# Sparse attention and a mixer MLP on one core: the later batches' instruction order, from fixed delays to a recorded reckoning of the engines

## The chip, the core and the metric

The kernel runs on one core of a Trainium2 chip. A core has a matrix engine (TensorE, PE in the profile), three engines for elementwise work (VectorE or DVE, ScalarE or ACT, GpSimd or POOL) and SyncE (SP), which issues most of the DMAs here. Each engine takes its own instructions strictly in the order in which the program lists them, and waits for others by semaphores. The metric is the device time of one execution in microseconds; lower is better.

## The reference

`q`, `k` and `v` are [4, 8, 768, 64] (batch, head, position, width of a head). Attention is masked by blocks of 32 positions.

```python
scores = scale * np.matmul(q, k.transpose(0, 1, 3, 2))      # scale = 1/8
mask = np.abs(blk_i - blk_j) <= 1                           # neighbours, first and last block,
mask = mask | (blk_i == 0) | (blk_j == 0) | (blk_i == n_blocks - 1) | (blk_j == n_blocks - 1)
...                                                         # and 3 sampled blocks for each block
attn = softmax(np.where(mask, scores, -1e9))
x = np.matmul(attn, v)        # heads side by side: [4, 768, 512]
h = x.transpose(0, 2, 1) @ U @ V                            # rank 32, over positions
u = x + h.transpose(0, 2, 1)
out = u + np.maximum(u @ w_ch1, 0.0) @ w_ch2                # 512 -> 2048 -> 512
```

## The kernel before

Heads are handled in pairs: 4 batches x 4 pairs make 16 pairs, numbered `i`. The scores of a pair are cut into nine **units** `u`, each 128 keys (or two halves of them) by 512 queries for both heads. A unit is a few matmuls into a double bank of PSUM (`psc`), one exp on ScalarE (`est<-psc`, 128 x 1024) and, in batches 1 to 3, one multiplication by a 0/1 mask on VectorE (`mask_mul`, `est<-est,m`). After the nine units of a pair come

- `values`: 72 small matmuls into `pav`, a reciprocal and a scaling on VectorE (`xs`), and a cast to 16 bits on GpSimd (`xh`);
- `mix_a_rows`: 12 matmuls into `pa` with `Ut` (from U), and two small VectorE steps (`a16`);
- `mix_h_rows`: 6 matmuls into `ph` with `Vd` (from V), an add on VectorE (`xf`), a cast on GpSimd (`uh`), and `turn_u`, a DMA that transposes `uh` into `uT`.

When all four pairs of a batch have their `uT`, its MLP can run: 16 blocks of the first layer (`w1`, tile `pt`), each in two phases of eight matmuls with a relu after the second, on ScalarE or VectorE (`tT<-pt`); then the second layer (`w2_rows`, tile `pch`, 192 matmuls for a batch), each third of it followed by an add on VectorE (`leave`, tile `of`) and a store. The matmuls of batches 0 to 2 use half of the rows each, two at a time; the last batch's (`w2`, and `w1` with whole rows) use all rows. Batch 0's attention is a part of its own (the head, its masks are added inside the matmul, and ScalarE sets its pace); its MLP runs beside batch 1's attention, and so on; the last MLP runs alone.

PSUM holds four double banks in the later part, numbered 0 to 3 and handed out by `double` and `give_back`: `psc`, `pt`, `pch`, `pav`, `pa` and `ph` all take one.

The order of every engine's instructions is that in which the Python code records them (`keep`). In before, the later batches are recorded in **groups of one unit**, numbered `gi`. Unit `gi` is recorded; then the masks of the units before it; when the ninth mask of a pair is recorded, its `values` goes one group later, `mix_a_rows` five and `mix_h_rows` eight groups later (`work`, `beside`); then a share of the running MLP (`run_fill`), such that it is used up when the next MLP opens. The MLPs open at fixed groups: 5 for the first, and then 16 groups after the last unit of the batch (`OPENS`, `LATE`). `clk` holds a reckoned time for each engine; it chooses banks, and ScalarE or VectorE for a relu.

```python
OPENS = [5]
for b in range(1, B):
    last = [n for n, gr in enumerate(groups) if (HP * b + HP - 1, NU - 1) in gr][0]
    OPENS.append(last + LATE)
...
work.append((gi + 1, steps[0]))      # values
beside.append((gi + 5, steps[1]))    # mix_a_rows
beside.append((gi + 8, steps[2]))    # mix_h_rows and turn_u
...
run_fill(sum(c for c, _, _ in fill) / (to_come[0] - gi))
```

Loads of `q`, `k` and `v` (`issue`) go out on SP three pairs ahead and are cast on GpSimd (`cast`) two pairs ahead; `turn_dma` transposes q and k of the next pair by DMA. U and V are loaded into a part of `w2t`'s space on SP, after the loads of pair 2, and copied into `Ut` and `Vt` on GpSimd at the start of pair 1 (`at_unit`, lines 877 and 883), ahead of the first `xh` casts.

Of the kernel before, what the change touches and what calls it, by code (L numbers as in the profile page):

```python
# [21 lines left out]
def kernel(  # L22
# [81 lines left out]
    clk = {"pe": 0.0, "act": 0.0, "dve": 0.0}  # L104
# [21 lines left out]
    def give_back(t, when):  # L126
        n = held.pop(id(t))[0]
        doubles[n] = (doubles[n][0], when + LAG)

# [296 lines left out]
    ready = {}  # L426
# [10 lines left out]
    def scores(i, u, est):  # L437
        psc = double("psc", len(exp_end) % 2 if i < HP else None)
        for g, q0, q1, at in parts(u):
            kc = slice(g * P, (g + 1) * P)  # L440
            for h in range(2):
                o = psc[:, h, at : at + q1 - q0]
                if i < HP:
                    s = i % 2
                    mm(o, ka[s][h][:, kc], qa[s][h][:, q0:q1], True, True)
                else:
                    qT, kT = (qkT[i, nm].rearrange(flat) for nm in "qk")
                    mm(o, kT[rows[h], kc], qT[rows[h], q0:q1], True, True)
        clk["pe"] += 0.22
        if i < HP:  # L450
            clk["pe"] = max(clk["pe"], exp_end[-2]) + 0.1
        keep(nc.scalar.activation(out=est, in_=psc, func=AF.Exp, scale=0.125))  # L452
        exp_end.append(run_on("act", 0.905))
        ready[id(est)] = exp_end[-1]
        give_back(psc, exp_end[-1])

    def mask_mul(u, est):
# [8 lines left out]
        run_on("dve", 0.8, ready[id(est)])  # L466
# [49 lines left out]
    def values(i, ests, xs, xh):  # L516
# [3 lines left out]
        for c in range(2):  # L520
            for h in range(2):
# [8 lines left out]
        rcp = misc.tile([P, 2, 6], FP32, tag="rcp", name="rcp")  # L530
        keep(nc.vector.reciprocal(out=rcp, in_=pv[:, :, :, D]))  # L531
        keep(
            nc.vector.tensor_tensor(  # L533
                out=xs.rearrange("p (c j) (h d) -> p c (j h) d", c=2, h=2),
                in0=pv[:, :, :, 0:D],
                in1=rcp[:, :, :, None].broadcast_to([P, 2, 6, D]),
                op=ALU.mult,
            )
        )
        give_back(pav, run_on("dve", 1.2))  # L540
        keep(nc.gpsimd.tensor_copy(out=xh, in_=xs))  # L541
# [11 lines left out]
    def mix_a_rows(xh, box):  # L553
# [8 lines left out]
        a16 = box["a"] = misc.tile([P, P], FP16, tag="a16", name="a16")  # L562
        keep(nc.vector.tensor_copy(out=a16, in_=pa[:, 0, 0:P]))
        keep(nc.vector.tensor_tensor(out=a16, in0=a16, in1=pa[:, 1, 0:P], op=ALU.add))
        give_back(pa, run_on("dve", 0.57))
# [27 lines left out]
    def mix_h_rows(i, a16, xs, uh):  # L593
# [3 lines left out]
        for j in range(3):  # L597
            for c in range(2):
# [4 lines left out]
        u = xfs[b][:, :, hp * P : (hp + 1) * P]  # L603
        keep(
            nc.vector.tensor_tensor(  # L605
                out=u.rearrange("p (c j) n -> p c j n", c=2),
                in0=xs.rearrange("p (c j) n -> p c j n", c=2),
                in1=ph[:, :, 0:HS].rearrange("p c (j n) -> p c j n", j=3),
                op=ALU.add,
            )  # L610
        )
        give_back(ph, run_on("dve", 0.9))
        keep(nc.gpsimd.tensor_copy(out=uh, in_=u))  # L613
# [18 lines left out]
    def mlp_steps(b):  # L632
# [7 lines left out]
        def relu(dst, pt):  # L640
            ends = {e: max(clk[e], clk["pe"]) + d for e, d in (("act", 0.81), ("dve", 0.95))}
            o = dst.rearrange("p (c n) -> p c n", c=2)
            i = pt[:, :, 0:HS]
            if ends["act"] <= ends["dve"]:
                keep(nc.scalar.activation(out=o, in_=i, func=AF.Relu))  # L645
                give_back(pt, run_on("act", 0.81))
            else:
                keep(nc.vector.tensor_scalar_max(out=o, in0=i, scalar1=0.0))
                give_back(pt, run_on("dve", 0.95))
# [26 lines left out]
        def leave(sc, nsc, n0, n1, pch):  # L676
            if sc % 2 == 0 and n0 == 0:
                pair[3] = opool.tile([P, 2, HD], FP32, tag="of", name="of")
            of = pair[3][:, sc % 2 : sc % 2 + nsc, n0:n1]
            keep(nc.vector.tensor_add(out=of, in0=xfs[b][:, sc : sc + nsc, n0:n1], in1=pch))  # L680
            keep(
                nc.sync.dma_start(
                    out=out[b].rearrange("(p t) d -> p t d", t=T)[:, sc : sc + nsc, n0:n1],
                    in_=of,
                )
            )

        def w2_rows(s0, phase, part):
# [4 lines left out]
            for jj in range(4 * part, 4 * part + 4):  # L693
# [9 lines left out]
            if phase == 0 and part == 3:  # L703
                pair[2] = half_done(last)
            if phase == 1 and part == 3:
                leave(s0, 2, 0, HD, pair[1])
                give_back(pair[1], run_on("dve", 1.2))

        def w2(sc, part, n0, n1):
# [10 lines left out]
            if part == 3:  # L720
                leave(sc, 1, n0, n1, pch)
                give_back(pair[1], run_on("dve", 0.6))

        if b < B - 1:
            for jj in range(NJJ):
                for phase in range(2):
                    steps.append((0.65, lambda jj=jj, ph=phase: w1(jj, ph, True), phase == 1))
            for s0 in range(0, T, 2):
                for phase in range(2):
                    for part in range(4):  # L730
                        steps.append(
                            (
                                0.87,
                                lambda s0=s0, ph=phase, part=part: w2_rows(s0, ph, part),
                                phase == 1 and part == 0,
                            )
                        )
            return steps

        for jj in range(NJJ):  # L740
            for c in range(2):
                steps.append((0.65, lambda jj=jj, c=c: w1(jj, c, False), False))
        for sc in range(T):
            cuts = [(0, HD)] if (b, sc) != (B - 1, T - 1) else [(0, 384), (384, HD)]
            for n0, n1 in cuts:
                for part in range(4):
# [4 lines left out]
                            False,  # L751
# [74 lines left out]
    def at_unit(i, u):  # L826
        if (i, u) in MASKS:
            mask_tiles(MASKS.index((i, u)))
        if i == 0:
            if u == 0:  # L830
# [14 lines left out]
                issue(2, "qk")  # L845
                cast(1, "q")
                cast(1, "k")
                cast(1, "v")
            if u == 1:
                issue(2, "v")  # L850
# [6 lines left out]
                )  # L857
            if u == 3:
                issue(3)
# [10 lines left out]
        if u == 0:  # L870
            issue(i + 3)
            if i == 1:
                for h in range(2):
                    for r in range(2):
                        at = h * D + r * R
                        keep(
                            nc.gpsimd.tensor_copy(
                                out=Ut[rows[r], :, at : at + R],
                                in_=uld[rows[r]].rearrange("p (t r) -> p t r", t=T),
                            )  # L880
                        )
                keep(
                    nc.gpsimd.tensor_copy(
                        out=Vt[0 : 2 * R, :, :],
                        in_=mvld.rearrange("r (p t) -> r t p", t=T),
                    )
                )
# [28 lines left out]

    fill = deque()
    state = {"debt": 0.0}

    def run_fill(us):  # L920
        state["debt"] += us
        n = 0
        while fill and state["debt"] > 0:
            if fill[0][2] and n and us < 1e6:
                break
            cost, fn, _ = fill.popleft()
            fn()
            n += 1
            state["debt"] -= cost
        if not fill:  # L930
            state["debt"] = min(state["debt"], 0.0)

    def pair_tail(i, ests, xs, xh):
        box = {}
        uh = xpool.tile([P, T, P], FP16, tag="uh", name="uh")

        def both_h():
            mix_h_rows(i, box["a"], xs, uh)
            turn_u(i, uh)

        return [
            lambda: values(i, ests, xs, xh),
            lambda: mix_a_rows(xh, box),
            both_h,
        ]

    stream = [(i, u) for i in range(HP, NPAIR) for u in range(NU)]
    SINGLE = 8
    groups = [[x] for x in stream]
    LATE = 16  # L950
    OPENS = [5]
    for b in range(1, B):
        last = [n for n, gr in enumerate(groups) if (HP * b + HP - 1, NU - 1) in gr][0]
        OPENS.append(last + LATE)
    for name in ("pe", "dve"):
        clk[name] = clk["act"]

    live = {}
    unmasked = deque()
    work = deque()  # L960
    beside = deque()
    gi = 0
    while gi < len(groups) or unmasked or work or beside:
        made = []
        if gi == 6:
            more_doubles("pav", 2)
        if gi == 7:
            more_doubles("ps", 3)
        for i, u in groups[gi] if gi < len(groups) else []:
            b, hp = divmod(i, HP)  # L970
            if u == 0:
                if hp == 0:
                    start_batch(b)
                live[i] = ([], *new_x())
            est = new_est()
            live[i][0].append(est)
            scores(i, u, est)
            made.append((i, u, est))
        while beside and beside[0][0] <= gi:
            beside.popleft()[1]()  # L980
        for _ in range(len(unmasked) if gi >= SINGLE else 2 if gi > OPENS[0] else 0):
            i, u, est = unmasked.popleft()
            mask_mul(u, est)
# [85 lines left out]
```

## Time and profile before

| | |
|---|---|
| median of 5 runs | 287.66 us (286.37, 286.54, 287.66, 288.18, 289.91) |
| the profiled execution | 286.54 us, its span 284.6 us |
| PE, DVE, ACT, POOL busy | 276.8, 179.0, 182.2, 88.7 us |
| granted clock of PE | 1.00 throughout |
| HBM read and written | 27.90 and 6.29 MB |

A row of groups gives the line of the code, the engine, the operation, the tiles (out<-in), how often it ran, its busy time in us and the mean of one in ns, and then how long the engine had been idle before it and what ended that. All matmuls carry the line of the helper `mm` (L146); they are told apart by their tiles. A row of the chain of waits or of a timeline begins with the start in us and the duration. A row of the busy times by stretch gives the stretch, its length, and the busy time of each engine with its instructions; PE's is the time in which any matmul was under way, waiting ones among them.

### The profile page before, as it was taken

Reading aid. Unit: us, or ns where it says so; the run is one execution under the profiler, and the core shown is the slowest. Engines: PE = TensorE matmul, PEld = TensorE weight load, DVE = VectorE, ACT = ScalarE, POOL = GpSimd, SP = SyncE. Lnnn points to the kernel's source line nnn. Section 1 sums busy time; section 2 is a strip of 40 time slices with the busy share of each in tenths; the row PEclk is TensorE's granted clock in tenths of the full one; section 3 lists DMA queues with packets and bytes.
Section 4 is the critical chain, followed back from the end, with each engine's and each line's share of the span. In section 5 each row is a group of like instructions: output and inputs, shape, how many; then the busy total and the mean of one; then the engine's idle time right before and its main releaser. Section 6 shows DMA issues by size and latency. Waiting matters only on the chain.

```text
span 284.6 us, 8075 instructions
## 1 busy us (share of the span) xinstructions
PE 276.8 (97%) x3509; PEld 165.4 (58%) x3509; DVE 179.0 (63%) x277; ACT 182.2 (64%) x204; POOL 88.7 (31%) x104
## 2 busy tenths in 40 slices
PE   8999998999999999999999999999999999999996
PEld 3576775565756565666565656565574644665443
DVE  5666768878896979888867576977857431000112
ACT  3699999889796867698867464878866000665000
POOL 1559863224353444526132251611111110000000
PEclk9999999999999999999999999999999999999999
DMA  5999999990547565879080566341100113100112
GB/s 150 305 314 258 236 240 268 269 253 6 90 164 110 203 153 186 130 221 215 20 216 33 104 223 117 42 132 29 30 3 3 28 75 104 74 0 2 74 74 74
DMA packets 45234, 37.19 MB, mean 131 GB/s; under 512 B 27144, under 2 KB 42832, under 8 KB 45200
## 3 DMA queue, kind: packets, MB, share of 16 engines
q1 hardware_dynamic: 42024, 32.26, 43.1%
q0 software_dynamic: 2688, 4.19, 8.2%
q8 instruction: 27, 0.44, 0.7%
q10 hardware_dynamic: 488, 0.24, 0.4%
q14 instruction: 7, 0.06, 0.1%
HBM read 27.90 MB, written 6.29 MB: 120 GB/s over the span
## 4 chain that ended last, share of the span: by engine, by line
PE 78%; ACT 10%; DMA 4%; DVE 2%; POOL 2%; issue 2%; SPq 0%; ACTq 0%; DVEq 0%; POOLq 0%
PE pch L146 29%; PE pt L146 26%; PE pav L146 10%; ACT est L452 9%; PE psc L146 8%; DMA kld<-in_k_dram 3%; DMA ka<-onehot_const 2%; PE pa L146 2%; PE warm L146 1%; PE ph L146 1%; ACT tT L645 1%; POOL w1t L393 1%; PE pturn L226 0%; DVE est L465 0%; PE pm L146 0%
## 5 line engine op out<-in xcount | busy, mean ns | idle before, releaser
L452 ACT ACTIVATE est<-psc 128x1024 f16<-128x1024 f32 x144 | 144.2, 1037 | 45.3 <-PE psc L146 44.0
L146 PE MATMUL pt<-uT,w1t 64*128 64x384 f16 (+1 forms) x896 | 93.9, 324 | 1.0 <-ACT est L452 0.9
L146 PE MATMUL pch<-w2t,tT 64*128 64x512 f16 (+3 forms) x688 | 91.5, 372 | 0.3
L465 DVE TENSOR_TENSOR est<-est,m 128x1024 f16<-128x1024 f16 x108 | 90.8, 880 | 0.9 <-ACT est L452 0.8
L146 PEld LDWEIGHTS <-w1t 64*128 64x128 f16 (+1 forms) x896 | 48.1, 94 | 36.4 <-PE pt L146 6.7
L645 ACT ACTIVATE tT<-pt 128x768 f16<-128x768 f32 x54 | 44.8, 829 | 29.8 <-PE pt L146 29.8
L146 PEld LDWEIGHTS <-tT 64*128 64x128 f16 (+1 forms) x688 | 37.9, 95 | 41.4 <-PE pch L146 3.4
L146 PEld LDWEIGHTS <-est 128*128 128x128 f16 x1152 | 41.4, 97 | 10.8 <-issue 4.9
L146 PE MATMUL pav<-vt,est 128*128 128x65 f16 x1152 | 44.5, 193 | 0.1
L680 DVE TENSOR_TENSOR of<-xf,pch 128x1024 f32<-128x1024 f32 (+3 forms) x16 | 15.2, 950 | 42.6 <-PE pch L146 42.6
L146 PE MATMUL psc<-qT,kT 64*128 64x512 f16 (+1 forms) x288 | 41.6, 324 | 0.3 <-ACT est L452 0.3
L541 POOL CAST xh<-xs 128x768 f16<-128x768 f32 x12 | 13.6, 1130 | 64.6 <-DVE xs L533 45.9
L613 POOL CAST uh<-xf 128x768 f16<-128x768 f32 x12 | 13.7, 1142 | 58.5 <-DVE xf L605 29.4
L146 PE MATMUL psc<-qa,ka 128*128 128x512 f16 (+1 forms) x96 | 21.8, 331 | 0.2
L146 PEld LDWEIGHTS <-kT 64*128 64x128 f16 x288 | 14.3, 94 | 11.8 <-issue 0.9
L531 DVE RECIPROCAL rcp<-pav 128x12 f32<-128x12 f32 x12 | 2.8, 233 | 25.4 <-PE pav L146 25.4
L605 DVE TENSOR_TENSOR xf<-xs,ph 128x768 f32<-128x768 f32 x12 | 11.4, 950 | 10.6 <-PE ph L146 10.6
L220 POOL CAST kst<-kld 128x768 f16<-128x768 f32 x15 | 16.5, 1101 | 3.4 <-PE psc L146 2.2
L220 POOL CAST qst<-qld 128x768 f16<-128x768 f32 x15 | 16.1, 1070 | 3.8 <-PE psc L146 2.0
L214 POOL CAST vt<-vld 128x768 f16<-128x768 f32 x16 | 15.1, 941 | 4.3 <-DMA vld<-in_v_dram 4.3
L533 DVE TENSOR_TENSOR xs<-pav,rcp 128x768 f32<-128x768 f32 x12 | 11.5, 958 | 1.2
L146 PEld LDWEIGHTS <-ka 128*128 128x128 f16 (+1 forms) x108 | 9.0, 98 | 3.4 <-issue 1.7
(61 smaller groups left out, 128.2 us busy)
## 6 DMA issues: line engine op xcount, KB each, us to landing
vld<-in_v_dram SPq DMA_DIRECT2D x16, 384.0 KB, 6.1
qld<-in_q_dram SPq DMA_DIRECT2D x15, 384.0 KB, 4.9
kld<-in_k_dram SPq DMA_DIRECT2D x15, 384.0 KB, 5.6
out_dram<-of SPq DMA_DIRECT2D x9, 512.0 KB, 4.5
w1t<-in_moe_w_ch_dram POOLq DMA_DIRECT2D x4, 512.0 KB, 8.4
w2t<-in_moe_w_ch_dram POOLq DMA_DIRECT2D x4, 512.0 KB, 18.1
out_dram<-of SPq DMA_DIRECT2D x5, 256.0 KB, 2.0
qld<-in_q_dram SPq DMA_DIRECT2D x1, 256.0 KB, 3.0
```

Source lines behind the costliest of these rows:

```text
L146: ins = nc.tensor.matmul(out, lhsT, rhs, start=start, stop=stop, skip_group_check=loose)
L214: nc.gpsimd.tensor_copy(out=vts[b % 2][:, 2 * hp : 2 * hp + 2, :, 0:D], in_=ld)
L220: keep(nc.gpsimd.tensor_copy(out=st.rearrange("p t h d -> p h t d"), in_=ld))
L393: nc.gpsimd.dma_start(out=w1t[:, cc, :], in_=moe_w_ch1[cc * P : (cc + 1) * P, :])
L452: keep(nc.scalar.activation(out=est, in_=psc, func=AF.Exp, scale=0.125))
L465: keep(nc.vector.tensor_tensor(out=o, in0=o, in1=m, op=ALU.mult))
L533: nc.vector.tensor_tensor(out=xs.rearrange("p (c j) (h d) -> p c (j h) d", c=2, h=2), in0=pv[:, :, :, 0:D], in1=rcp[:, :, :, None].broadca ...
L541: keep(nc.gpsimd.tensor_copy(out=xh, in_=xs))
L605: nc.vector.tensor_tensor(out=u.rearrange("p (c j) n -> p c j n", c=2), in0=xs.rearrange("p (c j) n -> p c j n", c=2), in1=ph[:, :, 0:HS]. ...
L613: keep(nc.gpsimd.tensor_copy(out=uh, in_=u))
L645: keep(nc.scalar.activation(out=o, in_=i, func=AF.Relu))
L680: keep(nc.vector.tensor_add(out=of, in0=xfs[b][:, sc : sc + nsc, n0:n1], in1=pch))
```

## The change

The loop over groups is replaced. The reckoning `clk` gets a fourth engine (`pool`), and what ScalarE and VectorE have to do is no longer recorded at once: `later` puts each exp, mask, relu, scaling and add on a list with the time from which it can start, and `run_engines` records them in the order in which the reckoned engines would take them (a relu on whichever is earlier). PE's steps are recorded one at a time: first, in this order, `mix_h_rows`, `mix_a_rows` and `values` if their input is reckoned ready and a bank free; then a unit, if ScalarE is no more than 0.5 us ahead and the MLP has earned it (`credit` against `rate()`, the MLP time left over the units left); then a step of the MLP; then a unit ahead of its turn; else the reckoned PE idles 0.05 us. An MLP opens as soon as the batch's four `uT` are reckoned to have landed.

```diff
+    def later(eng, first, fn, when=None):
+        count[0] += 1
+        when = clk["pe"] if when is None else when
+        tasks[eng].append((when + LAG, first, count[0], fn))
+
+    def run_engines(t):
+        while True:
+            best = None
+            for eng in ("act", "dve"):
+                for kind in (eng, "any"):
+                    for task in tasks[kind]:
+                        start = max(clk[eng], task[0])
+                        late = 0.15 if kind == "any" and eng == "dve" else 0.0
+                        key = (start + late, task[1], task[2])
+                        if start <= t and (best is None or key < best[0]):
+                            best = (key, eng, kind, task, start)
...
@@ scores, mask_mul, values, mix_a_rows, mix_h_rows, relu, leave: the part after the matmuls
+        def exp(eng):
+            keep(nc.scalar.activation(out=est, in_=psc, func=AF.Exp, scale=0.125))
+            exp_end.append(clk["act"] + 0.92)
+            give_back(psc, exp_end[-1])
+            if then is not None:
+                later("dve", 3, then, exp_end[-1])
+            return 0.92
...
-        run_on("dve", 0.8, ready[id(est)])
+        return 1.25 if clk["pool"] > clk["dve"] else 0.69
...
+        later("dve", 1, norm_both)
...
+        later("dve", 0, both)
...
+            keep(nc.gpsimd.tensor_copy(out=uh, in_=u))
+            turn_u(i, uh)
+            then(run_on("pool", 1.15, end) + 3.0)
+            return 0.96
+
+        later("dve", 1, add)
...
+            later("any", 1, run)
...
+            later("dve", 2, run)
@@ mlp_steps: the second layer in steps of half the size
-                    for part in range(4):
+                    for part in range(8):
+                        kind = ("open", "swap")[ph] if part == 0 else ""
...
@@ at_unit: U and V
+                for h in range(2):
+                    keep(nc.sync.dma_start(out=mvld[h * R : h * R + R], in_=moe_V))
+                keep(
+                    nc.sync.dma_start(
+                        out=uld, in_=moe_U.rearrange("(p t) r -> p (t r)", t=T)
+                    )
+                )
                 issue(2, "qk")
...
-            if i == 1:
...
+            if u == 3:
+                for r in range(2):
+                    at = r * R
+                    keep(
+                        nc.gpsimd.tensor_copy(
+                            out=Ut[rows[r]].rearrange("p t (h c) -> p t h c", h=2)[
+                                :, :, :, at : at + R
+                            ],
...
@@ the later batches
+    HEAD = 7
+    for gi in range(HEAD):
+        if gi == 6:
+            more_doubles("pav", 2)
+        next_unit(True)
...
+        if gi >= 5:
+            run_fill()
...
+    clk["pe"] = clk["dve"] = max(clk["act"], clk["pe"])
+    more_doubles("ps", 3)
+    for mask in early:
+        later("dve", 3, mask, 0.0)
...
+    def try_values():
+        if not do_v or len(masked.get(do_v[0], ())) < NU or h_done < do_v[0] - 2:
+            return False
+        if max(masked[do_v[0]]) > clk["pe"] or not free_double():
+            return False
...
+    def rate():
+
+        left = sum(c for c, _, _ in fill)
+        units = max(len(stream) - HP * NU * (B - 1 - opened), 0)
+        if opened < B - 1:
+            return max(left - 12.5, 0.0) / units if units else 1.2
+        return max(left - 14.5, 0.0) / max(units, 1)
+
+    def try_unit(due):
+        if not stream or state["out"] > 12 or not free_double():
+            return False
+        if clk["act"] > clk["pe"] + (0.5 if due else 1.0) or due and credit < rate():
+            return False
+        next_unit()
+        return True
+
+    def try_fill():
+        if not fill:
+            return False
+        kind = fill[0][2]
+        if kind == "open" and not free_double():
+            return False
+        if kind == "swap" and clk["pe"] < state["last"] + 0.2:
+            return False
+        return True
+
+    while stream or fill or do_v or do_a or do_h or opened < B:
+        run_engines(clk["pe"])
+        if not fill and opened < B and len(uT_at[opened]) == HP:
+            if max(uT_at[opened]) <= clk["pe"]:
+                fill.extend(mlp_steps(opened))
+                opened += 1
+        if try_h() or try_a() or try_values():
+            continue
+        if try_unit(True):
+            credit -= rate()
+            continue
+        if try_fill():
+            credit = min(credit + run_fill(), 3.0)
+            continue
+        if try_unit(False):
+            credit -= rate()
+            continue
+        clk["pe"] += 0.05
```

The instructions are the same in number on every engine, but for U's copies (two of twice the size for four) and the choice of engine for a few relus; what moves is their order. The first seven units of batch 1 (`HEAD`) are recorded by hand in both kernels; in the changed one their masks are held back until the seventh is recorded. U and V are loaded ahead of q, k and v of pair 2 and copied ahead of the casts of pair 2.

## The prediction

> **What bounds it now.** I read the page's shares first, then its groups, then busy time cut at the twelve starts of `values`, then the chain of waits and the timelines of ScalarE (ACT), VectorE (DVE) and GpSimd (POOL).
>
> ```profile
> PE 276.8 (97%) x3509; PEld 165.4 (58%) x3509; DVE 179.0 (63%) x277; ACT 182.2 (64%) x204; POOL 88.7 (31%) x104
> ...
> L452 ACT ACTIVATE est<-psc 128x1024 f16<-128x1024 f32 x144 | 144.2, 1037 | 45.3 <-PE psc L146 44.0
> L465 DVE TENSOR_TENSOR est<-est,m 128x1024 f16<-128x1024 f16 x108 | 90.8, 880 | 0.9 <-ACT est L452 0.8
> ```
>
> TensorE (PE) is busy for 97%, but a busy matmul may be waiting, so I build a floor from what back-to-back matmuls take in the chain:
>
> ```profile
> 57.26 1.33 PE pt L146 x16
> 58.58 2.38 PE pav L146 x72
> 67.09 2.02 ACT est L452 x2
> 69.50 1.30 PE pt L146 x16
> 70.80 0.22 PE psc L146 x2
> 78.70 1.84 ACT est L452 x2
> 80.57 1.18 DVE est L465
> 81.75 0.88 DVE tT L648
> 88.98 1.73 PE pch L146 x16
> ```
>
> So eight first-layer matmuls (`pt`, one phase) cost 0.655, eight `pch` 0.865, a score unit 0.217 (0.33 right after a `pav`), `pav` 2.38, `pa` 0.335, `ph` 0.168. Counted in PE's order from 48.03 us on, where the later batches begin to set the pace: 105 units, 96 phases of `pt`, 576 row-paired `pch`, 12 each of `pav`, `pa`, `ph`, the first batch's last turns, and the last MLP (20.9 + 20.8 in the chain) come to 227.0 us. The stretch lasts 233.8 (48.03 to 281.83). **All that reordering this stretch can win is 6.8 us.** Cut at the starts of `pav`, the excess over the floor is, in turn: 1.4, 1.2, 0.7, 0.3, 0.2, 0.2, 0.1, 0.6, 0.3, 0.0, 0.7, 0.6, 0.6. Nearly half lies in the first three cuts. What they look like:
>
> ```profile
> core 0: us, PE busy (x) PEld busy (x) DVE busy (x) ACT busy (x) POOL busy (x), PEclk, DMA share, GB/s
> 48.03:58.58 10.55, 10.11 (x119) 5.62 (x119) 9.71 (x20) 9.24 (x12) 1.66 (x2) 1.00 1.22 262
> 58.58:72.55 13.97, 13.30 (x213) 8.60 (x213) 10.94 (x16) 12.55 (x16) 5.54 (x5) 1.00 0.38 107
> 72.55:86.28 13.73, 13.46 (x212) 8.79 (x213) 12.37 (x17) 11.63 (x15) 6.17 (x5) 1.00 0.52 131
> ```
>
> There ACT works 33.4 of 38.25 us and DVE 33.0: with `pt` steps, each unit's exp (0.95 packed) meets a relu (0.83), and no bank of PSUM comes free in time. That is why the chain leaves PE for ACT at 67.09 and for ACT and DVE from 78.70 to 82.63. From 86 us on PE runs nearly gapless.
>
> **The change, part by part.**
>
> *Pacing and readiness (main loop, `rate`, `try_unit`, `try_fill`).* No arithmetic goes or comes: the counts on each engine are equal, so only the 6.8 us and the head are at stake. At the third `pav` both orders have issued 29 units and all 32 `pt` phases of the first MLP; the changed one has also issued 12 `pch` and 8 more (24 matmuls against 8), 1.7 us more PE work. ACT's work up to there is that of before plus one relu (15 of 16 on ACT, not 14): 33.4 + 0.8 = 34.2; DVE sheds 0.95. Floor there: 36.7 against 35.0. ACT idled 4.8 us in this stretch. If it idles as long, the stretch takes 34.2 + 4.8 = 39.0, an excess of 2.3 instead of 3.3: gain 1.0. If its idleness falls to 3 (two exps or relus are now queued ahead of each `pav`, which is when it starved: 1.42 and 2.10 us in its timeline after the first two), 37.2: excess 0.5, gain 2.8. Below nothing is possible too, if ACT starves more. I take 1.8, range -1 to +2.8.
>
> The later cuts: the order now puts 3, 15 and 14 first-layer phases of the second MLP into its three cuts, and 1, 17 and 14 of the third MLP, against 7, 18, 7 and 9, 16, 7. ACT's sums (9 exps x 0.95 and its relus x 0.83) are at most 14.4, in the cut with PE's 14.33, where 10 units stand; its neighbour has 16.08 beside 11.9. DVE's sums, with the mean mask of 0.88, are 9.9 to 12.6 beside 12.6 to 16.3 of PE. So none is over its PE for two cuts. The ten last excesses sum to 3.6; the cuts of pure second layer show that 0.1 to 0.3 remains whatever the order. Ten times 0.2, and 0.4 for that tight cut, is 2.4: gain 1.2, range -1.5 to +2.
>
> *Masks held back.* The first twelve masks now stand after both `xf` adds and the q/k turns. What that could cost is the first `pav`, which needs nine:
>
> ```profile
> 54.31 4.90 DVE L465 TENSOR_TENSOR est<-est,m 128x1024 f16<-128x1024 f16 x8
> 62.21 3.14 DVE L465 TENSOR_TENSOR est<-est,m 128x1024 f16<-128x1024 f16 x3
> ```
>
> Alone a mask takes 0.61, beside POOL casts 1.05. The turns come one `pt` phase earlier, so masks can start near 53.1 and nine end near 58.6; PE reaches that `pav` at 48.03 + 11.35 + 1.4 = 60.8. Nothing is lost; without that cover, 0.6 per mask.
>
> The Trainium skill's "SBUF — State Buffer" (Who interferes with whom) speaks against an order that schedules masks next to casts: a DVE instruction with two SBUF inputs and a GpSimd read exclude each other, the loser waiting for the whole instruction. By the rule a mask caught by a cast (0.83 alone) would take 0.61 + 0.83 = 1.44; the rows show 1.05 to 1.18, with the cast stretched to 1.28 as well. For some 54 casts the rule would put 45 us on DVE, the rows (0.88 - 0.61, times 108) 29. The row decides; by the rule one cut of DVE (12.6) would grow by at most 5 x 0.3 and reach 14.1, still under its PE (15.1).
>
> *Drains by need, smaller second-layer steps, `turn_u` with its add.* The recorded costs (exp 0.92, relu 0.81, mask 0.69 or 1.25, add 0.96, add to the cast 1.15) lie within 0.1 of the rows, so most orders hold. Halving the `pch` steps adds no matmul. `uT` is now needed sooner: from the end of the last `ph` of a batch the before trace takes 5.1 us (69.5 to 70.5 add, to 71.8 cast, 2.8 landing). PE has between that `ph` and the next batch's first `pt` 7.6, 7.8 and 7.35 us of work in the new order, where before the margin after landing was 3 to 7. An output add (1.21) stands ahead of the first of these on DVE: 6.3. Cost taken: 0; if the landing is 2 us later, 1 to 2 us at each of three openings. SP's and POOL's orders are otherwise those of before up to swaps of neighbours.
>
> *U and V earlier (head).* POOL now copies `Ut` and `Vt` ahead of q, k and v of pair 2, and SP loads them ahead of those three (1.15 MB).
>
> ```profile
> 15.72 0.83 POOL L220 CAST qst<-qld 128x768 f16<-128x768 f32 x1 [1.99 <-PE psc L146]
> ...
> 19.74 1.50 POOL L877 CAST Ut<-w2t 64x192 f16<-64x192 f32 x4 [0.31 <-DMA w2t<-in_moe_U_dram]
> 21.30 1.56 POOL L883 CAST Vt<-w2t 64x768 f16<-64x768 f32 x1
> 22.80 0.95 POOL L505 CAST xh<-xs 128x384 f16<-128x384 f32 x2
> ```
>
> In before this made POOL late: `pa` waited for `xh`, and ACT, which paces the head, idled 0.63 and 0.36. The loads took about 6 us to land; issued from 10.6 to 11.5 they land at 16.5 to 17.5. Then 2.9 us of copies, and `qst` is ready at 20.2 to 21.2, while PE turns it at 19.25: a wait of 1 to 2 us, of which ACT's queue covers 0.4. Against that POOL has both copies behind it, and the 0.99 of idleness goes. Net a gain of 0.4 to a loss of 0.6 us; I take a loss of 0.1, near the middle.
>
> *The tail* (281.83 to the end, last add and store) and the last MLP are unchanged.
>
> **Sum:** 1.8 + 1.2 - 0.1 = 2.9 us. The profiled execution took 286.54 (span 284.6), the second fastest of five with median 287.66. From the mean of the three fastest (286.86) I get 284.0, 1.3% below the median. About 1% is what a measurement here can tell from no change, so faster means below 284.8.
>
> **Rivals.**
> 1. *ACT still sets the w1 stretch.* It idles as before or more and the first cuts give 0; the rest gives 1.2 less 0.5 for the head: 286.2, within 1%. For it: 34.2 us of ACT work in 36.7, and DVE near it. Against: 1.7 us more cover.
> 2. *No slack at the joints, slower.* Every `values`, `pa` and `ph` is now placed when the reckoning has its input just ready; before, fixed delays of units stood there (DVE idled 1.80 and 1.18 ahead of its reciprocal). PE takes its queue in order, so an input that is d late stops everything behind it. Exps are reckoned at 0.92 and take 0.95 to 1.04. With d = 0.6 at twelve `pav`: 7.2 - 2.9 = 4.3 slower, 291.2. It cancels the gain at d = 0.24 and makes 1% at 0.48. Against: masks alone run 0.08 under their reckoning, and a wait of PE lets ACT catch up once, not twelve times. Late `uT` would show at the same place.
> 3. *More than forecast:* only the handover (1.4) and 0.1 per cut remain, the head wins 0.6: about 281.5.
>
> **How the numbers follow.** Forecast 0.42 (own range 282.0 to 284.7), rival 1 0.30, rival 2 0.20, rival 3 0.08. So faster 0.50, same 0.30, slower 0.20. Eight in ten: 280.5 to 289.5, which takes in half of rival 2.
>
> **What would show it.** Right: chain nearly all PE after 50 us, the cut to the third `pav` near 38 us for 1.7 us more work, and no DVE tail like 80.57. Wrong: PE waiting for `est<-est,m` at `pav`, for `xh` at `pa`, for the DMA of `uT` at a batch's first `pt`, or PE at 19 to 21 us waiting for `qst`.

## The result, and the profile after

The changed kernel takes 285.61 us (median of 31 runs, 284.24 to 287.58) against 287.69 for before (52 runs beside it, 285.69 to 292.01). The ratio is 0.9931, 95% interval 0.9911 to 0.9950: 2.0 us faster, between 1.4 and 2.6. The forecast was 284.0. The direction was right and the time lies in the wide range given with eight chances in ten (280.5 to 289.5), but outside the forecast's own (282.0 to 284.7): the gain was 0.7% where 1.3% of the median was forecast, under the bound of 1% that the forecast had set for "faster".

Part of the 2.0 us goes with the clock: of the runs of before beside the experiments, 37 of 100 were granted 0.988 to 0.994 and took 2.6 to 3.0 us longer by their medians, of those of the changed kernel 4 of 44, and where 0.999 or 1.00 was granted the medians are 286.4 and 286.8 for before against 285.4 and 285.5, only 1.0 to 1.4 us apart; why the shares differ is not shown.

The profiled execution took 284.76 us, its span 282.9, its granted clock 1.00. From its page, shares and the two costliest groups off PE:

```profile
PE 274.5 (97%) x3509; PEld 165.3 (58%) x3509; DVE 175.7 (62%) x275; ACT 184.0 (65%) x206; POOL 85.3 (30%) x102
...
L481 ACT ACTIVATE est<-psc 128x1024 f16<-128x1024 f32 x144 | 143.1, 1033 | 42.6 <-PE psc L174 41.1
L502 DVE TENSOR_TENSOR est<-est,m 128x1024 f16<-128x1024 f16 x108 | 87.9, 837 | 18.7 <-ACT est L481 17.3
```

DVE is now close behind ACT: it spends 17.3 us waiting for an exp before a mask, where before it was 0.8. Hardly anything waits for a mask any more. PE's share is the same 97%.

Busy time in the first three cuts at `pav`, and in the cuts that end at the tenth and eleventh:

```profile
core 0: us, PE busy (x) PEld busy (x) DVE busy (x) ACT busy (x) POOL busy (x), PEclk, DMA share, GB/s
46.92:60.10 13.18, 12.65 (x147) 6.90 (x147) 11.67 (x22) 11.69 (x15) 3.57 (x4) 1.00 1.17 248
60.10:73.26 13.16, 12.87 (x209) 8.28 (x209) 10.44 (x14) 11.23 (x14) 4.44 (x4) 1.00 0.32 101
73.26:86.58 13.32, 13.22 (x204) 8.56 (x205) 9.42 (x14) 11.51 (x15) 5.28 (x5) 1.00 0.59 150
177.72:194.50 16.78, 16.60 (x252) 10.33 (x253) 12.88 (x18) 13.20 (x16) 5.73 (x5) 1.00 0.35 83
194.50:209.70 15.20, 15.00 (x230) 9.48 (x231) 9.74 (x14) 12.88 (x16) 2.50 (x2) 1.00 0.08 15
```

**Where the time came from.** The later batches can be measured from the exp at which the head hands over to the last add. These are the rows (ACT's timeline, then the last row of the chain), first of before, then after:

```profile
48.45 1.94 ACT L452 ACTIVATE est<-psc 128x1024 f16<-128x1024 f32 x2 [0.26 <-PE psc L146]
```

```profile
281.86 0.29 DVE of L680
```

```profile
47.34 2.85 ACT L481 ACTIVATE est<-psc 128x1024 f16<-128x1024 f32 x3 [0.26 <-PE psc L174]
```

```profile
280.13 0.29 DVE of L746
```

The stretch is 233.41 us before and 232.79 after, **0.62 us shorter**. Four executions of this order, in four kernels or runs, gave 232.79, 232.80, 232.79 and 232.79. So one profile mostly serves to compare stretches to a tenth of a microsecond; `e9_swap_wait_timed` below shows an exception, and of before itself one profile is kept. The other 1.1 us between these two profiles is the earlier hand-over, 47.34 against 48.45. Over all profiles with U and V early it averages 0.4 (see the end), and 0.6 and 0.4 together are near the 1.0 to 1.4 of the medians at the full clock.

By cuts, the excess over the floor of the prediction (same costs, each kernel's own order) is as follows. The floor adds 0.11 to a unit right after a `pav`. After, other matmuls stand in four of these places and pay the same (a phase there takes 0.76, not 0.655), so 0.11 is put behind these `pav` too:

```profile
119.27 0.76 PE pt L174 x8
```

| cut | 1 | 2 | 3 | 4 | 5 | 6 | 7 | 8 | 9 | 10 | 11 | 12 | last | sum |
|---|---|---|---|---|---|---|---|---|---|---|---|---|---|---|
| before | 1.4 | 1.2 | 0.7 | 0.3 | 0.2 | 0.2 | 0.1 | 0.6 | 0.3 | 0.0 | 0.7 | 0.6 | 0.6 | 6.9 |
| after | 1.8 | 0.6 | 0.5 | 0.2 | 0.0 | 0.4 | 0.4 | 0.1 | 0.0 | 0.7 | 0.9 | 0.0 | 0.7 | 6.3 |

The waits of cuts 2, 3, 8 and 12 shrank as they should; cuts 1, 6, 7, 10 and 11 took most of it back. What cuts 1, 6, 10 and 11 contain that before did not is this, in the chain after:

```profile
53.07 1.30 PE pt L174 x16
...
58.34 0.22 PE psc L174 x4
58.56 0.67 PE pt L174 x7
59.23 0.05 issue
59.28 0.82 PE pt L174 x8
60.10 2.39 PE pav L174 x72
```

The first row is sixteen `pt` matmuls that end one block and begin the next: 1.30 us. The rows at 58.56 to 60.10 are the two phases of one block back to back: 0.67 + 0.05 + 0.82 = 1.54. The second phase adds into the same banks with the row halves swapped and waits (`half_wait`) until the last matmul of the first has ended. With a unit between the phases, a phase mostly takes its 0.65 to 0.68; back to back the pair costs 0.23 more. Before, `run_fill` broke off at each phase change, so none of 48 in the first layer stood back to back (3 of 9 in the second). After, 7 and 2 do: in cuts 1, 3, 6 and 10 one each, in cut 11 three, and two of the second layer in the last. They are not all: cut 7 grew by 0.3 without one, its cause not separated, and in cut 10 the chain also leaves PE for an exp, at 183.92.

### The profile page after: what moved, and what is told of

It is laid out like the page before. It is cut to its first block, busy times and chain, and to the rows that moved or that the text cites. A ratio compares the mean times of both kernels' runs of the same rounds, so it can differ in the third digit from the quotient of the medians.

```text
span 282.9 us, 8068 instructions
## 1 busy us (share of the span) xinstructions
PE 274.5 (97%) x3509; PEld 165.3 (58%) x3509; DVE 175.7 (62%) x275; ACT 184.0 (65%) x206; POOL 85.3 (30%) x102
## 4 chain that ended last, share of the span: by engine, by line
PE 81%; ACT 9%; DMA 5%; issue 1%; DVE 1%; POOL 1%; SPq 0%; ACTq 0%; DVEq 0%; POOLq 0%
PE pch L174 30%; PE pt L174 29%; PE pav L174 10%; ACT est L481 9%; PE psc L174 9%; DMA kld<-in_k_dram 3%; PE pa L174 1%; DMA w2t<-in_moe_U_dram 1%; PE ph L174 1%; DVE xh L524 0%; PE pturn L254 0%; POOL Ut L926 0%; DVE xs L572 0%; POOL qst L248 0%; POOL Vt L936 0%
## 5 line engine op out<-in xcount | busy, mean ns | idle before, releaser
L502 DVE TENSOR_TENSOR est<-est,m 128x1024 f16<-128x1024 f16 x108 | 87.9, 837 | 18.7 <-ACT est L481 17.3
L174 PE MATMUL pt<-uT,w1t 64*128 64x384 f16 (+1 forms) x896 | 96.3, 324 | 1.0 <-ACT est L481 0.3
L174 PE MATMUL pch<-w2t,tT 64*128 64x512 f16 (+3 forms) x688 | 92.5, 372 | 0.2
L705 ACT ACTIVATE tT<-pt 128x768 f16<-128x768 f32 x56 | 46.1, 829 | 29.5 <-PE pt L174 29.2
L174 PEld LDWEIGHTS <-tT 64*128 64x128 f16 (+1 forms) x688 | 38.7, 95 | 38.6 <-PE pch L174 2.8
L581 POOL CAST xh<-xs 128x768 f16<-128x768 f32 x12 | 11.4, 953 | 95.0 <-DVE xs L572 70.4
L174 PEld LDWEIGHTS <-kT 64*128 64x128 f16 x288 | 14.9, 94 | 11.4 <-issue 1.3
L242 POOL CAST vt<-vld 128x768 f16<-128x768 f32 x16 | 16.4, 1025 | 4.8 <-DMA vld<-in_v_dram 4.8
L248 POOL CAST qst<-qld 128x768 f16<-128x768 f32 x15 | 14.0, 936 | 4.7 <-PE pa L174 2.7
## 6 DMA issues: line engine op xcount, KB each, us to landing
w2t<-in_moe_w_ch_dram POOLq DMA_DIRECT2D x4, 512.0 KB, 19.2
```

The lines of the kernel that those rows point to most:

```text
L174: ins = nc.tensor.matmul(out, lhsT, rhs, start=start, stop=stop, skip_group_check=loose)
L242: nc.gpsimd.tensor_copy(out=vts[b % 2][:, 2 * hp : 2 * hp + 2, :, 0:D], in_=ld)
L248: keep(nc.gpsimd.tensor_copy(out=st.rearrange("p t h d -> p h t d"), in_=ld))
L502: keep(nc.vector.tensor_tensor(out=o, in0=o, in1=m, op=ALU.mult))
```

## The experiments

The theory: the order did remove ACT's waits, and phase changes back to back ate much of it. Rivals: ACT's load holds the first-layer stretches whatever the order; inputs come late at the joints (rival 2 of the prediction); the whole gain is the head's, from U and V.

### The two parts apart, and slack (timed on one chip)

`e1_uv_only` is before with only U and V earlier, `e2_order_only` the changed kernel with U and V at their old place.

```diff
 e1: at_unit of before
+                [loads of V, V, U]
                 issue(2, "qk")
...
             if u == 3:
+                [copies to Ut, Ut, Vt]
                 issue(3)
...              [the old loads and copies go]
```

> Before, with only the earlier loads and copies of U and V. Two readings of the two traces stand against each other. Reading A (the head's 1.1 us earlier hand-over is chance of that execution, since ScalarE's first exp already began at 7.78 instead of 9.54 us, ahead of anything the change touches; the move itself costs: ScalarE idles 1.59 us at 20.04 waiting for PE's turn of qst, against 0.63 and 0.36 saved): 0.3 to 0.8 us slower than before, ratio 1.001 to 1.003. Reading B (the move is what brings the head forward): 0.8 to 1.3 us faster, ratio 0.9955 to 0.997. In both PE should be seen waiting for the cast of qst near 19 us.

Measured: 0.9961 (0.9934 to 0.9988), 1.1 us faster, which is reading B and excludes A. In the profiled execution ACT's gap at `qst` was only 0.15 us; its first exp had come at 9.53. The stretch, in the order of before, is 233.99 here, 0.6 longer than before's (see masks beside casts, below).

> The changed kernel with U and V loaded and copied where they were before, so only the order of the later batches is new. Reading A: faster than the changed kernel by 0.3 to 0.8 us, that is 2.3 to 2.8 us faster than before, ratio 0.990 to 0.992. Reading B (the order is worth only the 0.6 us by which its stretch is shorter in the traces, 233.2 against 233.8): ratio 0.997 to 0.998.

Measured: 0.9944 (0.9911 to 0.9976), stretch 232.80. The interval touches both readings and decides neither; the stretches say that with U and V at the old place the order is worth 0.6 (233.41 to 232.80), and with U and V early 1.2 (233.99 to 232.79).

`e3_uv_copies_later` keeps the early loads but copies behind the casts of q and k of pair 2:

```diff
             if u == 6:
                 cast(2, "q")
                 cast(2, "k")
+                [copies to Ut, Ut, Vt, no longer at u == 3]
                 cast(2, "v")
```

> The changed kernel with U and V still loaded early, but their copies on GpSimd put behind the casts of q and k of pair 2 (recorded at unit 6 of pair 0 instead of unit 3), ahead of the cast of v. The turn of qst then no longer waits for the copies. If that wait is what the move costs (1.59 us of ScalarE idleness at 20 us, no other gap of the head over 0.4), the head ends 0.8 to 1.5 us earlier and the ratio to before is 0.988 to 0.991. If the wait is hidden later in the head (at the hand-over the chain goes through VectorE's last masks and turns), it equals the changed kernel, 0.993.

Measured: 0.9943 (0.9912 to 0.9974), no gain over the changed kernel; in its profile the hand-over came late, at 48.28. POOL's timeline shows why:

```profile
17.40 0.83 POOL L248 CAST qst<-qld 128x768 f16<-128x768 f32 x1 [3.87 <-DMA qld<-in_q_dram]
...
21.86 0.82 POOL L242 CAST vt<-vld 128x768 f16<-128x768 f32 x1
22.63 0.95 POOL L542 CAST xh<-xs 128x384 f16<-128x384 f32 x2
```

POOL idles 3.87 us for q of pair 2, which now lands behind U and V, and has the copies still to do; `xh` starts at 22.63, nearly as late as before (22.80), and ACT's gaps are now 0.91 us at 19.1 and 1.49 at 24.5. The changed kernel's place for the copies fills just that hole.

`e4_slack` asks for 0.6 us of slack at the joints:

```diff
-        if max(masked[do_v[0]]) > clk["pe"] or not free_double():
+        if max(masked[do_v[0]]) + SLACK > clk["pe"] or not free_double():
...
-        if not do_a or do_a[0][0] > clk["pe"] or not free_double():
+        if not do_a or do_a[0][0] + SLACK > clk["pe"] or not free_double():
...
-        if not do_h or do_h[0][0] > clk["pe"] or not free_double():
+        if not do_h or do_h[0][0] + SLACK > clk["pe"] or not free_double():
```

> The changed kernel with 0.6 us of slack asked of the reckoning before values, the U product and the V product may be placed. If inputs that come late at these joints (rival 2 of the prediction) ate the missing part of the gain, this is 1 to 3 us faster than the changed kernel, ratio 0.983 to 0.990. If ScalarE's share of the first-layer stretches sets what is left, it is within 0.5 us of the changed kernel, 0.992 to 0.995. The order found also shifts by a unit here and there, as it does with any constant.

Measured: 0.9918 (0.9892 to 0.9944), but its stretch is 233.32, 0.5 longer than the changed kernel's: in cuts 5 and 9 PE now waits about 1 us for an exp (the chain leaves it at 115.22 and 177.66). The better ratio is not the stretch's, and it is within the interval. Slack does not help, so missing slack did not hold the gain back: rival 2 falls.

### What the stretch is made of (one execution each)

`e5_nobreak` is before without the rule against phase changes back to back; 21 more of them, every cut's work the same but for a phase or two at its border:

```diff
-            if fill[0][2] and n and us < 1e6:
-                break
```

> Before, without the rule that a group of units may not run both phases of a first-layer block back to back (the line that breaks off the filling at a phase change is taken out). Back-to-back phase changes rise from 0 to 20 of 48 in the first layer and from 3 to 4 in the second. In the changed kernel's trace a back-to-back pair of phases takes 0.67 + 0.05 + 0.82 = 1.54 us against 1.31 for sixteen matmuls that change the block instead: 0.23 each. If that is the price of every such change, the stretch from the hand-over exp to the last add grows from 233.4 to 237.5 to 238.2 us. If ScalarE's waits hide it (its first-layer stretches are the tight ones in any case), the stretch grows by less than 1.5.

The stretch is 285.76 - 48.20 = 237.56, **4.15 us longer** for 21 of them. Its chain repeats the signature, and each of the 20 pairs in the first layer shows it:

```profile
82.86 0.67 PE pt L146 x7
83.53 0.05 issue
83.58 0.82 PE pt L146 x8
```

```profile
285.76 0.29 DVE of L680
```

So the price is real, but 4.15 / 21 is not it. Cut 1 alone grew by 1.06 for one change, because there the turns of q and k have lost their cover and PE waits for VectorE:

```profile
53.33 0.56 DVE qT L813
53.88 0.47 DVE kT L813
```

The other 20 changes cost 3.1, **0.15 each**: the full 0.23 and more in cuts 6, 7 and 12, but 0.1 on average in cuts 2, 3, 8 and 11. Waits that were there anyway hide about a third. Whole executions: 290.31 us against 287.24.

`e6_swap_wait` makes the reckoning avoid them:

```diff
-        if kind == "swap" and clk["pe"] < state["last"] + 0.2:
+        if kind == "swap" and clk["pe"] < state["last"] + (0.4 if stream else 0.2):
```

> The changed kernel with one constant of its reckoning altered: a phase change directly after the phase before it costs 0.4 us of waiting in the reckoning instead of 0.2, so that a unit is put between. Back-to-back changes fall from 7 to 0 in the first layer and from 2 to 1 in the second. If these are what kept the stretch at 232.8, it falls by 1.4 to 1.9, to 230.9 to 231.4. If ScalarE's load in the first-layer stretches sets the time, the waits come back at the banks and the stretch stays within 0.5 of 232.8.

With 8 fewer, the stretch is 279.69 - 48.12 = 231.57, 1.22 shorter than the changed kernel's: a little less than expected, well past the 0.5 that ACT's load would have allowed, and 0.15 for each change, as in `e5_nobreak`. The order shifts elsewhere too, so it is the agreement of the two that counts.

`e7_half_relu` takes load from ACT, the order unchanged:

```diff
-            o = dst.rearrange("p (c n) -> p c n", c=2)
-            i = pt[:, :, 0:HS]
+            o = dst[:, 0:HS]
+            i = pt[:, 0, 0:HS]
...              [w2_rows and w2 read the written half twice]
```

> The changed kernel, same order, with relus on half of their columns (the second layer reads the written half twice; half of the first layer's result is left out). This takes about 0.38 us from each of 56 relus on ScalarE and from those on VectorE, some 5 us in the first 40 us of the stretch. If ScalarE's load is what holds the first-layer stretches, the excess there (2.9 us in the first three cuts) falls by at least 1.5 and the whole stretch by 2 to 3.5. If what is left is PE's own (phase changes back to back, the first read after values, the hand-over), it falls by less than 0.7.

The stretch falls by 0.72 to 232.07, the first three cuts together by 0.28. **ACT's load is not what was left there.** It still holds a little: 0.28, and 0.1 to 0.2 each in cuts 6, 7, 10 and 11.

`e8_half_mask` takes load from DVE:

```diff
-            o = est
-            m = m01[:, 2 * tr + kind, None, 0:QA].broadcast_to([P, 2, QA])
+            o = est[:, :, 0 : QA // 2]
+            m = m01[:, 2 * tr + kind, None, 0 : QA // 2].broadcast_to([P, 2, QA // 2])
...              [the third kind of unit likewise]
```

> The changed kernel, same order, with the masks of the later batches on half of their columns (half of the masking is left out). About 0.3 us less for each of 108 masks on VectorE. VectorE waits 17 us for exps as it is, so if ScalarE or PE sets the time the stretch changes by less than 0.4. If late masks at values hold PE (rival 2 of the prediction), it falls by 1 or more.

It falls by 0.44, to 232.35, spread thinly over the cuts, 0.1 at most in one: just past the first expectation and far from the second. Late masks at `values` are not what holds PE.

### A better version, timed beside the changed kernel (on one chip)

> The changed kernel itself once more, on the same chip and beside the same runs of before, as the yardstick for the other three: 0.993 within 0.002, its stretch 232.79 within 0.05 as in every profile of this order so far.

The changed kernel again: 0.9941 (0.9907 to 0.9974), median 285.53, stretch 232.79.

> The version with the phase change reckoned at 0.4 us, timed. Its stretch was 1.84 us shorter than before's and 1.22 shorter than the changed kernel's. With the changed kernel at 0.993, this comes to 0.988 to 0.990 if the head is as in the changed kernel; if the head's spread hides it, 0.991 to 0.993.

0.9917 (0.9880 to 0.9953), median 284.87, the lowest median of all versions, though its interval overlaps that of the changed kernel. Its stretch was 232.44 here, not 231.57: the cut in which the third MLP opens took 16.41 instead of 15.55. The chain there leaves PE:

```profile
173.07 4.66 DMA uT<-uh
177.72 0.04 issue
177.76 0.34 PE pt L174 x2
```

The transposing DMA of the batch's last `uT` took 4.66 us, where 2.8 is the median, and PE waited for it. In `e6_swap_wait`, the same program, the same DMA landed after 2.74 us and held nothing. In both the loads of k and v were issued 1.3 and 1.9 us behind it, so these loads alone do not explain it; the cause stays open. This is the late `uT` that the prediction feared, 0.9 us at one opening, in an order that leaves it less time.

`e11_wait_old_uv` is the same with the old place of U and V:

> The version with the phase change at 0.4 and U and V loaded and copied where they were before: same stretch, 231.57 within 0.1, old head. Its distance to the timed version with the early U and V is what the early U and V are worth: 0.3 to 0.6% (0.8 to 1.7 us) if the head gains what the medians of the earlier runs left for it, under 0.1% if the trace's early start was chance.

0.9937 (0.9900 to 0.9975), median 285.66, stretch 232.47, with the same late `uT` (4.70). The early U and V are thus worth 0.8 us by medians and 0.6 by ratios, but the intervals overlap.

`e10_wait_measured` keeps the 0.4 us and sets the reckoned costs to those of the traces:

```diff
-            exp_end.append(clk["act"] + 0.92)
+            exp_end.append(clk["act"] + 0.955)
...
-        return 1.25 if clk["pool"] > clk["dve"] else 0.69
+        return 1.05 if clk["pool"] > clk["dve"] else 0.62
```

> The same with the reckoning's exp at 0.955 us instead of 0.92 and its mask at 0.62 or 1.05 instead of 0.69 or 1.25, as the traces have them. If a truer reckoning matters (inputs late at the joints), the stretch falls by another 0.5 to 1 below 231.57. If it does not, it is within 0.3 of that, by chance of the order found.

0.9927 (0.9899 to 0.9955), stretch 232.50: a truer reckoning gained nothing. `uT` came in time here; what made cut 9 long is that PE waited for three exps, until 180.94, ahead of a `values`. The chain goes straight from an exp to `pav`, without the mask that an input would need, so it seems to be a bank that came late.

## Why the prediction was right, and where it was not

The direction was right and its mechanism in part: waits for ACT and DVE did shrink. The size was not. Of the 3.0 us forecast for the stretch 0.6 came; the head gained where a small loss was forecast, and the clock's part in the 2.0 us was no one's forecast. That the time lies in the range owes something to its width and to these two.

**The bound of the gain** (6.8 us of excess in the stretch) holds: the best order here, `e6_swap_wait`, won 1.84.

**Pacing and readiness, first three cuts: forecast 1.8, measured 0.3** (excess 3.3 to 2.9). The mechanism worked where it could: cuts 2 and 3, where ACT and DVE had held PE, gave 0.8. In the prediction's own term, ACT's idleness, 4.8 before, was to stay or to fall towards 3; it was 5.2 (39.66 us less 34.43 of work). Two sizes were off. The first: the hand-over of cut 1 (1.4 us) was counted as winnable, though rival 3 itself names it as what remains; the order there is written by hand in both kernels, and the chain after runs through the same two exps from 47.3 to 49.3. The second: the floor prices every phase of eight at 0.655, in whatever place. In cuts 1 and 3 a phase change stands back to back, at up to 0.23 each.

**The later cuts: forecast 1.2, measured 0.3** (3.6 to 3.3). The step that failed is the floor's one price for every phase, wherever it stands: five phase changes came to stand back to back in the first layer and one fewer in the second, 0.6 at the net 0.15 and 0.9 at the 0.23 of the chain. `e6_swap_wait`, which has none left in the first layer and one in the second, brings these cuts to 2.4, the forecast's own figure. The new order, which the prediction used for counts per cut, would have shown the phases of one block side by side; I counted phases and did not look at their neighbours.

**ACT as the bound of what remains** (the prediction's frame for these cuts and its rival 1) fell with `e7_half_relu`: 0.72 us for 0.34 off each relu on ACT.

**Masks held back: nothing lost**, as forecast; PE reached the first `pav` at 60.10 (forecast 60.8, with a hand-over 1.1 later) straight from a `pt`. On masks beside casts `e1_uv_only` gave one more number. Two early masks with one cast among them took 1.91 us, against 1.28 for the same two in before; the second mask took 1.31 instead of 0.69 and the cast 1.03 instead of 0.83. By the Trainium skill's "SBUF — State Buffer" (Who interferes with whom) the loser waits until the other instruction is done: this mask began 0.77 before the cast's end and would take 0.77 + 0.69 = 1.46, so the measured 1.31 is near the rule and a little under it. The prediction's 1.44 was for a mask that begins together with a cast. The late masks held the turn of q and k, so that this kernel's first cut was 0.6 longer.

**`uT` nearer to its need: cost 0 in the changed kernel**, as taken. Its price when it bites was seen in `e9_swap_wait_timed`.

**U and V: forecast a loss of 0.1, measured a gain**, of a size that stays open. The wait for `qst` came as described:

```profile
15.73 1.07 POOL L926 CAST Ut<-w2t 64x384 f16<-64x384 f32 x2 [1.17 <-DMA w2t<-in_moe_U_dram]
16.85 1.55 POOL L936 CAST Vt<-w2t 64x768 f16<-64x768 f32 x1
18.36 0.82 POOL L248 CAST qst<-qld 128x768 f16<-128x768 f32 x1
```

```profile
7.78 3.84 ACT L481 ACTIVATE est<-psc 128x1024 f16<-128x1024 f32 x4 [0.54 <-PE psc L174]
11.77 6.68 ACT L481 ACTIVATE est<-psc 128x1024 f16<-128x1024 f32 x7 [0.16 <-PE psc L174]
20.04 24.89 ACT L481 ACTIVATE est<-psc 128x1024 f16<-128x1024 f32 x26 [1.59 <-PE psc L174]
```

ACT's timeline has the gap of 1.59 before 20.04, and then 26 exps without one, where before it idled 0.63 and 0.36. Two sizes were off. The loads landed at 15.6, not 16.5 to 17.5, so `qst` was ready at 19.2, not 20.2 to 21.2. And the wait costs only where the head began early: of the nine profiles with U and V early (leaving out `e3_uv_copies_later`), the first exp came at 7.6 to 7.8 in seven (then the gap was 1.5 to 2.2) and at 9.5 in two (then 0.15 to 0.26), and the hand-over fell between 47.3 and 48.1, with no clear tie to either. With U and V at the old place all four began at 9.2 to 9.5. The two programs profiled twice repeat their first exp (7.78 and 7.78, 7.62 and 7.56), so it may go with the program; why is not shown. Means of the profiled hand-overs are 47.72 with U and V early and 48.15 at the old place (four): 0.4 us. Medians and ratios give 0.6 to 1.1 (`e1`, `e9` against `e11`), each with an interval of about 0.8 or more. That the head gained is likely; how much is not settled.

**The rivals.** By its time, rival 1 (within 1%) described the outcome, but not by its cause. Rivals 2 and 3 did not come. (Rival 3's own terms, 6.8 less 1.4 and 1.2 and with 0.6 for the head, make 282.1, not 281.5.)

## What to carry to other kernels

When a floor is built from the cadence of matmuls, price the places where one kind follows another, above all two groups that add into the same banks and wait for each other; with 8 of the 9 taken out the stretch gained 1.84 us instead of 0.62. A busy engine with no waits in the table of waits can still lose microseconds in such seams, and only rows of the chain that do the same work in unequal time show them. Where one part of a kernel repeats to hundredths and another scatters by a microsecond, compare the first part within profiles and leave the second to medians, and look at the granted clock of the runs behind a median.

## What was not expected of the hardware

The order of 230 us of work on five engines, once fixed, ran in the same time to 0.01 us in four executions; another order took 231.57 us once and 232.44 once, when one DMA landed late. The head does not repeat: the first exp came at 7.6 or at 9.5 us in kernels that differ only later, and one program handed over at 47.34 once and at 48.02 once. A phase change back to back costs PE 0.23 us in the chain and 0.15 of the stretch on average. A transposing DMA took 2.74 us in one execution and 4.66 in another of the same program, with the same two loads of 384 KB issued directly behind it.
